# Making a table of angles by sine instead of by doubling, in a kernel that mixes an SSM and an MLP

## The chip, the cores and the metric

The kernel runs on one core of a Trainium2 chip. The metric is the device time of one execution in microseconds (us); the number for a kernel is the median of three such times. Before the change it was 549.61 us (549.30 to 549.72).

## The reference

Two branches read the same input x (2048 tokens of 1024 features, bf16) and are mixed by a gate per token. Cut to what matters:

```python
dt = exp(log_dt)
Lam_bar = exp(dt * Lam)                       # complex, one per channel, 1024 channels
B_bar = ((Lam_bar - 1) / Lam)[:, None] * Bmat
Bu = einsum("bld,pd->blp", x, B_bar)
for t in range(L):                            # 2048 steps
    h = Lam_bar * h + Bu[:, t]
a = 2 * einsum("blp,dp->bld", hs, Cmat).real + x * Dskip
b = gelu(layernorm(x) @ w1 + b1) @ w2 + b2
g = sigmoid((x * gate_w).sum(-1))
out = g * a + (1 - g) * b
```

## The kernel before, in words

The recurrence is split into size and angle. Lam_bar is R·exp(i·theta). In each stretch of T = 256 time steps the products Bu are turned by exp(-i·theta·t), so that a real scan with the factor R on VectorE (DVE, line 1471) is enough, and the result is turned back. For this a table of cos(theta·t) and sin(theta·t) is needed for t = 0 to 255 and 1024 channels: 128 partitions by 8 channels by 256 times, in f32 (region `E1`). From it the bf16 tables in `TABR` are written (lines 1056, 1058, 1071, 1073), which the DVE multiplications of the scan stage read (`ssm`, lines 1457 and 1460).

The table is made from theta in these steps. DVE brings dt·Im(Lam)/2pi into one turn (lines 966 to 969: `phi`, `ki`, `kf`, `ttr`), and a second copy that is a quarter turn ahead (lines 970 to 973), and clips both (975, 976). ScalarE (ACT) takes the sine of both (lines 977, 978). Then a recurrence of doublings on DVE: lines 996 to 998 give cos and sin of theta·2^k for k = 1 to 8 (three instructions each, 8 columns wide), and line 1024 doubles the table seven times (six instructions each, 8 to 512 columns wide), from column 128 upward, starting from a one and a zero that lines 1029 and 1031 set. ACT mirrors the upper half to the lower half (line 1047).

Matrix products run on TensorE (PE) in the groups of a Winograd-like scheme: a group has seven products `p1` to `p7` (lines 1090 and 1092), 4 matmuls of 512 columns each in the first stage. ACT copies PSUM banks out for it (`snap`, lines 1114 and 1115) and seeds a bank from another (line 1130); `p6` of a group waits for the seed, `p3` for the snap named s5. DVE writes other results out (line 1267) and makes sums and differences of operands in 16 bit (line 1180). The first group products read DVE's differences of x.

The order of the instructions on every engine is written by a planner in the kernel: it lists all steps with their dependencies, durations and priorities, simulates them, computes from the end backward when each step must start at the latest, subtracts a small random lead from that (`MIX` is the seed and the size of the lead), and orders each engine by it. Each engine then runs its list strictly in order, with semaphore waits. PE's list comes out in the order in which the code names the products.

Of the kernel before, what the change touches and what calls it, by code (L numbers as in the profile page):

```python
# [14 lines left out]
TWO_PI = 2.0 * math.pi  # L15
# [11 lines left out]
MIX = (12, 0.4)  # L27
# [19 lines left out]
def c_dve(N):  # L47
    return 0.09 + N / 960.0
# [547 lines left out]
def V(t, off, dims, npart=128):  # L596
    ps = 1
    for s in t.shape[1:]:
        ps *= s
    return bass.AP(t, off, [[ps, npart]] + [[a, b] for (a, b) in dims])  # L600


def build(nc, A_x, A_Lambda_re, A_Lambda_im, A_B_re, A_B_im, A_C_re, A_C_im, A_log_dt, A_Dskip,
# [25 lines left out]
    with es:  # L629
# [105 lines left out]
        for nm in ("DTC", "A", "TH", "R", "PHI", "KFX", "TTR", "T2", "KF2", "T3", "C1", "S1", "UR", "UI",  # L735
                   "Q", "Q2", "INV", "N1", "N2", "N3", "N4", "E20R", "E20I", "CC", "SS", "NMS"):
            alloc_cols(nm, PT)
        for k in range(1, LT + 1):
            alloc_cols("MC%d" % k, PT)
            alloc_cols("MS%d" % k, PT)  # L740
        col["MC0"] = col["C1"]
        col["MS0"] = col["S1"]
        b_cst["MC0"] = bc("C1")
        b_cst["MS0"] = bc("S1")
# [5 lines left out]
        def C(name, j=0, n=1):  # L750
            return V(CST, col[name] + j, [(1, n)])
# [201 lines left out]
        def dv(name, fn, reads, writes, dur=0.12, eng="dve", prio=(2.0, 0)):  # L953
            return g.add(eng, dur, prio, fn, reads=[bc(r) for r in reads], writes=[bc(w) for w in writes], name=name)
# [1043 lines left out]
```

## Time and profile before

| what | value |
|---|---|
| median of three runs | 549.61 us |
| the profiled execution, its own time | 549.65 us |
| span of its instructions | 547.8 us |
| PE busy | 541.2 us, 99% |
| DVE busy | 505.1 us, 92%, 870 instructions |
| ACT busy | 279.0 us, 51%, 466 instructions |
| POOL busy | 86.0 us, 16%, 146 instructions |
| granted TensorE clock | full in all 40 slices |

The span runs from the first to the last instruction of the program; 1.85 us of the time lie outside of it. Busy time is the union of an engine's instructions. PE's matmuls are pipelined, each is shown with 0.38 us although the next one starts 0.216 us later, and 47 of 2628 matmul records are missing, while all 2628 weight loads (PEld) are there. A weight load stands in the trace some 0.2 us ahead of its matmul, since it is fetched while the matmul before still runs.

### The profile page before, as it was taken

The numbers are of one execution on the slowest core, as the hardware profiler recorded it, in microseconds if no ns is written. First come the engines' busy times: TensorE is split into PE (matmuls) and PEld (weight loads), VectorE is DVE, ScalarE is ACT, GpSimd is POOL, SyncE is SP. The second block draws the span as 40 slices with busy tenths as digits, with TensorE's granted clock in tenths as the row PEclk, the third lists the DMA queues.
The fourth block names the chain that finished last, engine by engine and source line by source line (L and its number), as shares of the span: only waits on it lengthen the run. The fifth ranks groups of instructions, "written<-read, shape, count | busy, mean of one in ns | idle before, by whom it ended". The sixth has DMA issues, their size and how long they took to land.

```text
span 547.8 us, 7420 instructions
## 1 busy us (share of the span) xinstructions
PE 541.2 (99%) x2581; PEld 249.9 (46%) x2628; DVE 505.1 (92%) x870; ACT 279.0 (51%) x466; POOL 86.0 (16%) x146
## 2 busy tenths in 40 slices
PE   8999999999999999999999999999999999999998
PEld 6444444444444444444444444444444444444444
DVE  5997898999999999999999999999999999989884
ACT  3657988877764257763347762247663322111110
POOL 0134455610001110001210001120001100022000
PEclk9999999999999999999999999999999999999999
DMA  9999999959965155634778772977767997679621
GB/s 265 196 341 234 272 267 273 372 174 323 274 116 191 78 193 186 217 107 171 257 291 231 268 186 46 223 124 238 239 157 143 220 330 282 223 252 271 224 100 59
DMA packets 116448, 117.99 MB, mean 215 GB/s; under 512 B 72626, under 2 KB 94898, under 8 KB 115386
## 3 DMA queue, kind: packets, MB, share of 16 engines
q1 hardware_dynamic: 103792, 71.59, 46.7%
q0 software_dynamic: 12480, 45.90, 27.4%
q8 instruction: 21, 0.34, 0.3%
q14 instruction: 17, 0.14, 0.1%
q10 hardware_dynamic: 138, 0.02, 0.0%
HBM read 55.87 MB, written 45.37 MB: 185 GB/s over the span
## 4 chain that ended last, share of the span: by engine, by line
PE 98%; DMA 1%; issue 1%; SPq 0%; DVE 0%
PE ps L1092 72%; PE ps L1090 24%; DMA ar<-in_A_x_dram 1%; PE ps L935 0%; PE ps L1333 0%; PE ps L862 0%; PE ps L1161 0%; PE ps L838 0%; PE ps L912 0%; SPq L894 0%; SPq L808 0%; DVE ar L1783 0%; PE ps L947 0%
## 5 line engine op out<-in xcount | busy, mean ns | idle before, releaser
L1092 PE MATMUL ps<-ar 128*128 128x512 f16 (+1 forms) x1804 | 414.6, 379 | 2.2
L1092 PEld LDWEIGHTS ps<-ar 128*128 128x128 f16 (+1 forms) x1844 | 180.0, 98 | 218.5 <-ACT ar L1114 0.6
L1090 PE MATMUL ps<-ar 128*128 128x512 bf16 (+1 forms) x601 | 149.0, 379 | 0.3
L1180 DVE TENSOR_TENSOR ar<-ar 128x512 f16<-128x512 bf16 (+6 forms) x224 | 141.9, 663 | 0.8 <-ACT ar L870 0.3
L1090 PEld LDWEIGHTS ps<-ar 128*128 128x128 bf16 (+1 forms) x608 | 59.3, 98 | 71.1
L1471 DVE TENSOR_TENSOR_SCAN ar<-cst,init,ar 128x256 bf16<-128x256 f32 x128 | 88.6, 736 | 0.3
L1114 ACT ACTIVATE ar<-ps 128x512 f32<-128x512 f32 x102 | 60.4, 595 | 54.5 <-PE ps L1090 38.4
L1130 ACT ACTIVATE ps<-ps 128x512 f32<-128x512 f32 x67 | 38.9, 581 | 77.4 <-PE ps L1090 66.9
L1457 DVE TENSOR_TENSOR ar<-ar 128x2048 bf16<-128x2048 bf16 x64 | 77.1, 1218 | 0.0
L1115 ACT ACTIVATE ar<-ps,cst 128x512 f32<-128x512 f32 x32 | 22.0, 687 | 45.8 <-PE ps L1092 22.9
L1578 ACT ACTIVATE ar<-ps,cst 128x512 bf16<-128x512 f32 x56 | 38.4, 687 | 13.5 <-PE ps L1092 13.0
L1667 ACT ACTIVATE ar<-ps,cst 128x512 f32<-128x512 f32 x32 | 21.8, 687 | 45.0 <-PE ps L1092 45.0
L1582 DVE TENSOR_TENSOR ar<-ps,ar 128x512 f32<-128x512 f32 x56 | 38.1, 684 | 5.2 <-PE ps L1092 4.5
L1460 DVE TENSOR_TENSOR ar<-ar 128x1024 bf16<-128x1024 bf16 x64 | 42.3, 685 | 0.2
L1584 ACT ACTIVATE ar<-ar,cst 128x512 bf16<-128x512 f32 x56 | 39.7, 713 | 3.6 <-DVE ar L1582 3.6
L1198 POOL DMA_DIRECT2D scr_u<-ar x32 | 24.7, 774 | 56.2 <-ACT ar L1262 19.8
L1796 DVE SCALAR_TENSOR_TENSOR ar<-ps,cst,ar 128x512 bf16<-128x512 f32 x31 | 23.0, 747 | 8.8 <-PE ps L1092 8.7
L1489 POOL DMA_DIRECT2D scr_h<-ar x16 | 9.0, 563 | 125.4 <-DVE ar L1460 108.5
L1670 DVE SCALAR_TENSOR_TENSOR ar<-ps,cst,ar 128x512 f32<-128x512 f32 x32 | 23.7, 745 | 4.3 <-PE ps L1092 4.2
L1267 DVE TENSOR_TENSOR ar<-ps,ar 128x512 bf16<-128x512 f32 x30 | 20.5, 685 | 6.2 <-PE ps L1092 5.7
L1681 POOL DMA_DIRECT2D scr_ac<-ar x12 | 10.3, 888 | 78.6 <-DVE ar L1471 26.0
L1679 POOL DMA_DIRECT2D scr_ac<-ar x16 | 8.5, 532 | 79.6 <-DVE ar L1180 36.9
(121 smaller groups left out, 229.7 us busy)
## 6 DMA issues: line engine op xcount, KB each, us to landing
scr_ac<-ar POOLq DMA_DIRECT2D x28, 512.0 KB, 5.2
ar<-in_A_x_dram SPq DMA_DIRECT2D x32, 256.0 KB, 5.9
scr_u<-ar POOLq DMA_DIRECT2D x32, 256.0 KB, 5.1
ar<-scr_u SPq DMA_DIRECT2D x16, 512.0 KB, 4.7
scr_h<-ar POOLq DMA_DIRECT2D x16, 512.0 KB, 4.6
ar<-scr_h SPq DMA_DIRECT2D x8, 1024.0 KB, 6.6
ar<-in_B_w_dram SPq DMA_DIRECT2D x14, 512.0 KB, 4.7
ar<-in_B_w_dram SPq DMA_DIRECT2D x8, 896.0 KB, 7.6
```

Source lines behind the costliest of these rows:

```text
L1090: ins = e.matmul(V(PS[bk], 0, [(1, n)]), st[i].ap, mv[i].ap, start=(i == 0), stop=(i == K - 1))
L1092: ins = e.matmul(V(PS[bk], 0, [(1, n)]), st[i].ap, mv[i].ap, start=False, stop=(i == K - 1), skip_group_check=True)
L1114: return e.activation(o.ap, V(PS[bk], 0, [(1, 512)]), AF.Copy)
L1130: g.add("act", c_act(512), (pb[0], q - 2), lambda e: e.activation(V(PS[b], 0, [(1, 512)]), V(PS[a], 0, [(1, 512)]), AF.Copy), reads=[b_ps[ ...
L1180: g.add("dve", c_tt16(n), (pb[0], q), lambda e: e.tensor_tensor(o.ap, a.ap, b.ap, op), reads=[a, b], writes=[o], name=nm).slack = slack
L1198: g.dma((1.0, q), lambda e: e.dma_start(out=US[pt // 4, :, 4 * pr:4 * pr + 4, r0:r0 + T], in_=evv.ap), 2 * 128 * CH * 2, ssem("us", 2 * ks ...
L1457: g.add("dve", c_tt16(UE), pri(i), lambda e: e.tensor_tensor(o.ap, a.ap, tbl.ap, ALU.mult), reads=[a, tbl], writes=[o], name=nm + tag)
L1460: g.add("dve", c_tt16(UE // 2), pri(i), lambda e: e.tensor_tensor(o.ap, a.ap, b.ap, op), reads=[a, b], writes=[o], name=nm + tag)
L1471: lambda e, pt=pt, ri=ri, vin=vin, go=go: e.tensor_tensor_scan(go.ap, Cb("R", pt, T), vin.ap, V(INIT, pt * 2 + ri, [(1, 1)]), ALU.mult, AL ...
L1578: g.add("act", c_act(512, ap_operands=1), (10.0, q + 1), lambda e: e.activation(o.ap, V(PS[bk], 0, [(1, 512)]), AF.Gelu_apprx_tanh, bias=C ...
L1582: g.add("dve", c_dve(512), (10.0, q - 2), lambda e: e.tensor_tensor(sv.ap, V(PS[bk], 0, [(1, 512)]), sv.ap, ALU.add), reads=[b_ps[bk], sv] ...
L1584: g.add("act", c_act(512, psum=False, ap_operands=1), (10.0, q + 3), lambda e: e.activation(o.ap, sv.ap, AF.Gelu_apprx_tanh, bias=C("B1", ...
```

## The change

The sine and cosine are taken directly. One phase per channel (`TTR`, in turns) is multiplied on DVE by the column numbers 0 to 127, a row that GpSimd (POOL) writes by doubling into `ONESF`; it is brought into one turn by adding and subtracting 12582912, which rounds, and by one subtraction. ACT takes the sine of the whole upper half (1024 columns for each partition), and the cosine as 1 - 2·sin(half the angle)²: a sine, a square and a copy with scale and bias, all 1024 columns wide. The few columns that the other formulas need (theta, 128 theta and 256 theta) come from the same five steps on 24 columns. The 24 instructions of lines 996 to 998, the 42 of line 1024, the two memsets and the quarter-turn copy go. The planner's seed goes from 12 to 23.

```diff
-MIX = (12, 0.4)
+MIX = (23, 0.4)
...
-        dv("t2", ...0.25 added...)   dv ki2, kf2, t3, ttr_cl, t3_cl
-        dv("sin", lambda e: e.activation(C("S1", 0, n8), C("TTR", 0, n8), AF.Sin, scale=TWO_PI), ["TTR"], ["S1"], dur=0.3, eng="act", prio=P0).slack = 5.0
-        dv("cos", lambda e: e.activation(C("C1", 0, n8), C("T3", 0, n8), AF.Sin, scale=TWO_PI), ["T3"], ["C1"], dur=0.3, eng="act", prio=P0).slack = 5.0
+        PTURN = TWO_PI * (1.0 - 3e-7)
+        RND = 12582912.0
+        dv("x1", lambda e: e.tensor_copy(C("X1", 0, n8), C("TTR", 0, n8)), ["TTR"], ["X1"])
+        dv("x2", lambda e: e.tensor_scalar(C("X2", 0, n8), C("TTR", 0, n8), float(T // 2), None, ALU.mult), ["TTR"], ["X2"])
+        dv("x3", lambda e: e.tensor_scalar(C("X3", 0, n8), C("TTR", 0, n8), float(T), None, ALU.mult), ["TTR"], ["X3"])
+        dv("xk", lambda e: e.tensor_scalar(C("XK", 0, 3 * n8), C("X1", 0, 3 * n8), RND, RND, ALU.add, ALU.subtract), ["X1", "X2", "X3"], ["XK"])
+        dv("xr", lambda e: e.tensor_tensor(C("X1", 0, 3 * n8), C("X1", 0, 3 * n8), C("XK", 0, 3 * n8), ALU.subtract), ["X1", "X2", "X3", "XK"], ["X1"])
+        dv("sin", ...24 columns, AF.Sin...)  dv sinh, sinq (Square), cos (Copy)
...
-        for k in range(LT):
-            dv("cs%d" % k, ...)
-            dv("ms%d" % k, ...)
-            dv("mc%d" % k, ...)
...
-        g.add("dve", 0.12, PT1, lambda e, v=v: e.memset(v.ap, 1.0), writes=[v], name="e1r0")
-        g.add("dve", 0.12, PT1, lambda e, v=v: e.memset(v.ap, 0.0), writes=[v], name="e1i0")
+        g.add("pool", 0.2, P0, lambda e: e.memset(V(ONESF, 0, [(1, 1)]), 0.0), reads=[b_ident], writes=[b_ones], name="iota0")
         for k in range(LT - 1):
             n = 1 << k
-            tt("e1.%da" % k, ...)   and five more
+            g.add("pool", 0.3, P0, lambda e, n=n: e.tensor_scalar(V(ONESF, n, [(1, n)]), V(ONESF, 0, [(1, n)]), 1.0, float(n), ALU.mult, ALU.add), reads=[b_ones], writes=[b_ones], name="iota%d" % n)
+        ph = V(CST, col["TTR"], [(1, PT), (0, TH)])
+        g.add("dve", c_dve(PT * TH), PT1, lambda e: e.tensor_tensor(up0.ap, V(ONESF, 0, [(0, PT), (1, TH)]), ph, ALU.mult), ..., name="e1x")
+        g.add("dve", 0.75, PT1, lambda e: e.tensor_scalar(lo0.ap, up0.ap, RND, RND, ALU.add, ALU.subtract), ..., name="e1k")
+        g.add("dve", c_dve(PT * TH), PT1, lambda e: e.tensor_tensor(up0.ap, up0.ap, lo0.ap, ALU.subtract), ..., name="e1r")
+        g.add("act", ca, PT1, lambda e: e.activation(up1.ap, up0.ap, AF.Sin, scale=PTURN), ..., name="e1s")
+        g.add("act", ca, PT1, lambda e: e.activation(lo1.ap, up0.ap, AF.Sin, scale=PTURN / 2), ..., name="e1h")
+        g.add("act", ca, PT1, lambda e: e.activation(lo1.ap, lo1.ap, AF.Square, scale=math.sqrt(2.0)), ..., name="e1q")
+        g.add("act", ca, PT1, lambda e: e.activation(up0.ap, lo1.ap, AF.Copy, scale=-1.0, bias=1.0), ..., name="e1c")
```

The change takes lines out, so a line behind it has a smaller number now: 1114, 1130, 1180, 1262 and 1267 of before are 1106, 1122, 1172, 1254 and 1259.

DVE, where the phases are ready (from `ttr`, line 969 before and 964 now, to the first operand sums). Before:

```order
L969 TENSOR_TENSOR cst<-cst 128x8
L970 TENSOR_SCALAR cst<-cst 128x8
L975 TENSOR_SCALAR cst<-cst 128x8
L971 CAST ki<-cst 128x8
L972 CAST cst<-ki 128x8
L973 TENSOR_TENSOR cst<-cst 128x8
L976 TENSOR_SCALAR cst<-cst 128x8
L1180 TENSOR_TENSOR ar<-ar 128x512 x2
L1180 TENSOR_TENSOR ar<-ar 128x2048
```

Now:

```order
L964 TENSOR_TENSOR cst<-cst 128x8
L967 COPY cst<-cst 128x8
L968 TENSOR_SCALAR cst<-cst 128x8
L969 TENSOR_SCALAR cst<-cst 128x8
L1027 TENSOR_TENSOR ar<-onesf,cst 128x8x128
L1172 TENSOR_TENSOR ar<-ar 128x512
L1172 TENSOR_TENSOR ar<-ar 128x2048
```

The six small steps of the quarter turn have become three (`x1` to `x3`), and `e1x` (L1027), 1024 columns wide, stands ahead of the operand sums.

DVE, behind those sums, with the first results of group u1.0 written out (L1267, now L1259). Before:

```order
L1267 TENSOR_TENSOR ar<-ps,ar 128x512
L997 SCALAR_TENSOR_TENSOR cst<-cst 128x8
L996 TENSOR_TENSOR cst<-cst 128x16
L1267 TENSOR_TENSOR ar<-ps,ar 128x512
L998 TENSOR_TENSOR cst<-cst 128x8
L1024 TENSOR_TENSOR ar<-ar,cst 128x8
```

Now:

```order
L970 TENSOR_SCALAR cst<-cst 128x24
L1259 TENSOR_TENSOR ar<-ps,ar 128x512
L971 TENSOR_TENSOR cst<-cst 128x24
L1028 TENSOR_SCALAR ar<-ar 128x8x128
L1259 TENSOR_TENSOR ar<-ps,ar 128x512
L1029 TENSOR_TENSOR ar<-ar 128x8x128
L1172 TENSOR_TENSOR ar<-ar 128x512
L1259 TENSOR_TENSOR ar<-ps,ar 128x512
L1172 TENSOR_TENSOR ar<-ar 128x512 x4
L1259 TENSOR_TENSOR ar<-ps,ar 128x512
```

The doublings no longer stand between the results; `xk`, `xr` (L970, L971) and the wide `e1k`, `e1r` (L1028, L1029) do.

ACT, from the snaps of groups u1.0 and u2.0 (L1114, now L1106) to the seed of group u0.1 (L1130, now L1122). Before:

```order
L1114 ACTIVATE ar<-ps 128x512 x2
L977 ACT_TABLE_LOAD
L977 ACTIVATE cst<-cst 128x8
L978 ACTIVATE cst<-cst 128x8
L1114 ACTIVATE ar<-ps 128x512 x2
L1130 ACTIVATE ps<-ps 128x512
L1262 ACTIVATE ar<-ps 128x512
L1114 ACTIVATE ar<-ps 128x512 x2
L1262 ACTIVATE ar<-ps 128x512 x2
L1130 ACTIVATE ps<-ps 128x512
```

Now, without the last two rows of that stretch, which are `e1c` (L1034) and the seed:

```order
L1106 ACTIVATE ar<-ps 128x512 x4
L1031 ACT_TABLE_LOAD
L1031 ACTIVATE ar<-ar 128x8x128
L1122 ACTIVATE ps<-ps 128x512
L1032 ACTIVATE ar<-ar 128x8x128
L973 ACTIVATE cst<-cst 128x24
L1254 ACTIVATE ar<-ps 128x512
L974 ACTIVATE cst<-cst 128x24
L1106 ACTIVATE ar<-ps 128x512 x2
L975 ACTIVATE cst<-cst 128x24
L1033 ACTIVATE ar<-ar 128x8x128
L1254 ACTIVATE ar<-ps 128x512 x2
```

The load of the sine's table stands two snaps later, and the wide `e1s` (L1031) now stands ahead of the seed of group u3.0, `e1h` (L1032) and two small ones ahead of its snaps, `e1q` (L1033) and `e1c` ahead of the seed of u0.1. PE's own list is the same in both kernels.

## Rows read from the trace of the kernel before

**Rows 1.** Chain that ended last, by engine, and PE's own waits (total, times, longest).
```profile
PE 98%; DMA 1%; issue 1%; SPq 0%; DVE 0%
...
PE ps L882 <- DVE ar L1031: 1.2, 1, 1.2
PE ps L838 <- DMA ar<-in_A_x_dram: 0.2, 1, 0.2
```

**Rows 2.** Timeline of the first and last microseconds: start, us, engine, line, what.
```profile
0.91 0.27 DVE L885 MEMSET ar<- 128x256 uint32 x1 [0.91 <-PEq L1983]
...
543.34 1.93 PE L1161 MATMUL ps<-ar 128*128 128x256 bf16 x24
```

**Rows 3.** Timeline from 104.5 us.
```profile
104.53 0.53 PEld L1092 LDWEIGHTS ps<-ar 128*128 128x128 f16 x3
...
104.81 1.28 DVE L1267 TENSOR_TENSOR ar<-ps,ar 128x512 bf16<-128x512 f32 x2
...
105.60 0.99 PEld L1092 LDWEIGHTS ps<-ar 128*128 128x128 bf16 x6 [0.55 <-issue]
```

**Rows 4.** Groups of lines on DVE that go: count, busy us, mean ns.
```profile
L1024 DVE TENSOR_TENSOR ar<-ar,cst 128x8 f32<-128x8 f32 (+6 forms) x28 | 7.2, 304 | 0.0
L1024 DVE TENSOR_TENSOR ar<-ar 128x8 f32<-128x8 f32 (+6 forms) x14 | 4.0, 304 | 0.0
```

**Rows 5.** DVE groups of one shape each, near to what is added.
```profile
L1180 DVE TENSOR_TENSOR ar<-ar 128x4096 f16<-128x4096 bf16 x4 | 9.1, 2284 | 0.0
L1307 DVE TENSOR_SCALAR ar<-ar,cst 128x1024 bf16<-128x1024 bf16 x16 | 8.6, 581 | 1.9 <-POOL cst L1302 1.8
...
L1024 DVE TENSOR_TENSOR ar<-ar,cst 128x512 f32<-128x512 f32 x4 | 2.6, 684 | 0.0
L1024 DVE TENSOR_TENSOR ar<-ar,cst 128x256 f32<-128x256 f32 x4 | 1.4, 419 | 0.0
```

**Rows 6.** Timeline of DVE, 15 to 30 us.
```profile
15.71 0.17 DVE L970 TENSOR_SCALAR cst<-cst 128x8 f32<-128x8 f32 x1
...
17.07 6.31 DVE L1180 TENSOR_TENSOR ar<-ar 128x512 f16<-128x512 bf16 x9 [0.30 <-ACT ar L870]
23.29 0.69 DVE L1267 TENSOR_TENSOR ar<-ps,ar 128x512 bf16<-128x512 f32 x1
...
29.94 0.68 DVE L1267 TENSOR_TENSOR ar<-ps,ar 128x512 bf16<-128x512 f32 x1
```

**Rows 7.** Timeline of PE, 20.5 to 39 us.
```profile
21.36 1.46 PE L1092 MATMUL ps<-ar 128*128 128x512 f16 x6
...
30.07 3.62 PE L1092 MATMUL ps<-ar 128*128 128x512 f16 x15
...
38.04 1.25 PE L1092 MATMUL ps<-ar 128*128 128x512 f16 x5
```

**Rows 8.** ACT groups of one shape: wide copies, and the sine of 8 columns.
```profile
L1056 ACT ACTIVATE ar<-ar 128x1024 bf16<-128x1024 f32 x2 | 2.1, 1048 | 0.0
...
L977 ACT ACTIVATE cst<-cst 128x8 f32<-128x8 f32 x1 | 0.2, 208 | 0.0
```

**Rows 9.** Timeline of ACT, 22 to 27 us.
```profile
22.43 0.60 ACT L1114 ACTIVATE ar<-ps 128x512 f32<-128x512 f32 x1 [0.27 <-PE ps L1092]
23.04 1.28 ACT L977 ACT_TABLE_LOAD   x1
24.34 0.21 ACT L977 ACTIVATE cst<-cst 128x8 f32<-128x8 f32 x1
...
25.95 0.60 ACT L1114 ACTIVATE ar<-ps 128x512 f32<-128x512 f32 x1 [0.27 <-PE ps L1092]
```

**Rows 10.** Timeline and groups of POOL: last memset, first DMA, dearest small operation.
```profile
1.32 0.10 POOL L1003 MEMSET init<- 128x16 f32 x1
20.73 1.72 POOL L1198 DMA_DIRECT2D scr_u<-ar  x2 [19.30 <-DMA ar<-in_A_x_dram]
...
L1301 POOL TENSOR_TENSOR cst<-cst 128x4 f32<-128x4 f32 x4 | 5.1, 1268 | 0.2
```

More of the change, by code (lines that the diff above doesn't have):

```diff
@@ L734, in build @@
         assert ncol[0] == NROW
-        for nm in ("DTC", "A", "TH", "R", "PHI", "KFX", "TTR", "T2", "KF2", "T3", "C1", "S1", "UR", "UI",
+        for nm in ("DTC", "A", "TH", "R", "PHI", "KFX", "TTR", "T2", "KF2", "T3", "UR", "UI",
                    "Q", "Q2", "INV", "N1", "N2", "N3", "N4", "E20R", "E20I", "CC", "SS", "NMS"):
             alloc_cols(nm, PT)
[L738 to L744, printed above, removed]
+        for nm in ("C1", "MC%d" % (LT - 1), "MC%d" % LT, "S1", "MS%d" % (LT - 1), "MS%d" % LT, "X1", "X2", "X3", "XK", "XK2", "XK3", "XH", "XH2", "XH3"):
+            alloc_cols(nm, PT)
         alloc_cols("MHALF", TT)
@@ new lines, in build @@
+        dv("xk", lambda e: e.tensor_scalar(C("XK", 0, 3 * n8), C("X1", 0, 3 * n8), RND, RND, ALU.add, ALU.subtract), ["X1", "X2", "X3"], ["XK"])
+        dv("xr", lambda e: e.tensor_tensor(C("X1", 0, 3 * n8), C("X1", 0, 3 * n8), C("XK", 0, 3 * n8), ALU.subtract), ["X1", "X2", "X3", "XK"], ["X1"])
+        trig_s, trig_c = ["S1", "MS%d" % (LT - 1), "MS%d" % LT], ["C1", "MC%d" % (LT - 1), "MC%d" % LT]
+        dv("sin", lambda e: e.activation(C("S1", 0, 3 * n8), C("X1", 0, 3 * n8), AF.Sin, scale=PTURN), ["X1"], trig_s, dur=0.3, eng="act").slack = 5.0
@@ L979, in build @@
+        dv("sinh", lambda e: e.activation(C("XH", 0, 3 * n8), C("X1", 0, 3 * n8), AF.Sin, scale=PTURN / 2), ["X1"], ["XH"], dur=0.3, eng="act").slack = 5.0
+        dv("sinq", lambda e: e.activation(C("XH", 0, 3 * n8), C("XH", 0, 3 * n8), AF.Square, scale=math.sqrt(2.0)), ["XH"], ["XH"], dur=0.3, eng="act")
+        dv("cos", lambda e: e.activation(C("C1", 0, 3 * n8), C("XH", 0, 3 * n8), AF.Copy, scale=-1.0, bias=1.0), ["XH"], trig_c, dur=0.3, eng="act")
         dv("ur0", lambda e: e.tensor_tensor(C("UR", 0, n8), C("R", 0, n8), C("C1", 0, n8), ALU.mult), ["R", "C1"], ["UR"])
@@ L1027, in build @@
         TH = T // 2
-        v = w1(0, TH, 1)
-        g.add("dve", 0.12, PT1, lambda e, v=v: e.memset(v.ap, 1.0), writes=[v], name="e1r0")
-        v = w1(1, TH, 1)
-        g.add("dve", 0.12, PT1, lambda e, v=v: e.memset(v.ap, 0.0), writes=[v], name="e1i0")
+        up0, up1, lo0, lo1 = w1(0, TH, TH), w1(1, TH, TH), w1(0, 0, TH), w1(1, 0, TH)
+        g.add("pool", 0.2, P0, lambda e: e.memset(V(ONESF, 0, [(1, 1)]), 0.0), reads=[b_ident], writes=[b_ones], name="iota0")
         for k in range(LT - 1):
@@ L1041, in build @@
-            tt("e1.%de" % k, PT1, o0, o0.ap, t0.ap, ALU.add, [o0, t0], dc)
-            tt("e1.%df" % k, PT1, o1, o1.ap, t1.ap, ALU.subtract, [o1, t1], dc)
+            g.add("pool", 0.3, P0, lambda e, n=n: e.tensor_scalar(V(ONESF, n, [(1, n)]), V(ONESF, 0, [(1, n)]), 1.0, float(n), ALU.mult, ALU.add), reads=[b_ones], writes=[b_ones], name="iota%d" % n)
+        ph = V(CST, col["TTR"], [(1, PT), (0, TH)])
+        g.add("dve", c_dve(PT * TH), PT1, lambda e: e.tensor_tensor(up0.ap, V(ONESF, 0, [(0, PT), (1, TH)]), ph, ALU.mult), reads=[b_ones, bc("TTR")], writes=[up0], name="e1x")
@@ new lines, in build @@
+        g.add("dve", 0.75, PT1, lambda e: e.tensor_scalar(lo0.ap, up0.ap, RND, RND, ALU.add, ALU.subtract), reads=[up0], writes=[lo0], name="e1k")
+        g.add("dve", c_dve(PT * TH), PT1, lambda e: e.tensor_tensor(up0.ap, up0.ap, lo0.ap, ALU.subtract), reads=[up0, lo0], writes=[up0], name="e1r")
+        ca = c_act(PT * TH, psum=False)
+        g.add("act", ca, PT1, lambda e: e.activation(up1.ap, up0.ap, AF.Sin, scale=PTURN), reads=[up0], writes=[up1], name="e1s")
+        g.add("act", ca, PT1, lambda e: e.activation(lo1.ap, up0.ap, AF.Sin, scale=PTURN / 2), reads=[up0], writes=[lo1], name="e1h")
@@ L1043, in build @@
+        g.add("act", ca, PT1, lambda e: e.activation(lo1.ap, lo1.ap, AF.Square, scale=math.sqrt(2.0)), reads=[lo1], writes=[lo1], name="e1q")
+        g.add("act", ca, PT1, lambda e: e.activation(up0.ap, lo1.ap, AF.Copy, scale=-1.0, bias=1.0), reads=[lo1], writes=[up0], name="e1c")
         NTAB = PT * T
```

18 lines of the change are left out of this document (removed).

## The prediction

> **What bounds the kernel now.** I read the chain that ended last first, since it names the engine whose work adds up to the time: 98% of it is PE [rows 1]. Next come PE's own waits. There are two in the whole execution, 1.2 us at the start and 0.2 us for a DMA in the opening [rows 1]. The last matmuls stand at 543.34 us and run 1.93 us, so PE ends at 545.27, and 2.57 us of output DMA follow to the end of the span [rows 2]. From the second of them on to 545.3 us PE has work in hand nearly all the time; its list is the same in both kernels. The time can fall only by the few tenths that PE does lose, and rise only where a result from another engine reaches PE later than the matmul in front of it ends.
>
> DVE is 92% busy, which invites the reading that work taken from DVE is time won. The chain says otherwise: DVE has 0% of it [rows 1]. A busy engine that always delivers before PE asks costs nothing.
>
> The third reading is of the weight loads, which show small delays that the waits leave out. At 104.53 us three loads follow each other at 0.216 us, the third thus at 104.96, and the next was due at 105.17 but stands at 105.60 [rows 3]. It is 0.43 us late, of which some 0.2 us are covered by the lead of a load over its matmul, so PE lost about 0.23 us. What it waited for is the first of the two DVE results from 104.81 us on [rows 3].
>
> **The change, part by part.**
>
> What goes from DVE: the 42 instructions of the doublings, 7.2 + 4.0 = 11.2 us [rows 4], and 32 small ones (24 for the multiples of theta, six for the quarter turn and two memsets), at the 0.17 us of such an instruction [rows 6] some 5.4 us. Together 16.6 us. What comes: five small ones, 0.85 us, and three wide ones. Line 1024 took 684 ns for 512 columns and 419 for 256 in f32 [rows 5], 1.035 ns a column, so `e1x` and `e1r` with 1024 columns take 684 + 512 x 1.035 = 1214 ns each. For `e1k`, one f32 input and two constants, the nearest row is the tensor-scalar of 1024 columns in bf16, 581 ns [rows 5]; I take 0.65 us. Added: 0.85 + 2.43 + 0.65 = 3.9 us, net -12.7 us of DVE time. On PE's path that is zero, except at 105 us. There DVE hands over late; its work for the scan can begin earlier now, and the 0.23 us should go. This is the only gain that I count. Its bounds are 0 (the new order may be as tight there) and 0.23; I take 0.23, since the removed work is many times that.
>
> `e1x` stands ahead of the operand sums that PE waits for. Before, the first replaced step started at 15.71 us and the sums at 17.07, after 0.30 us of waiting for ACT [rows 6]. Now three small independent steps take 15.71 to about 15.95 (such instructions follow each other at 0.08 us when they don't depend), `e1x` runs to 15.95 + 1.21 = 17.16, and the next may enter 0.08 us before that end. So the sums start at about 17.1, where ACT lets them start anyway. The second difference of x is needed at 21.36 [rows 7]. In the new order it is the fourth of the sums. The nine sums, four of 2048 columns and five of 512, took 6.31 us [rows 6], about 1.13 and 0.34 us each, so it ends at 17.1 + 2 x 0.34 + 2 x 1.13 + 0.1 = 20.1. That is 1.2 us early: zero. Behind the sums DVE now has `xk`, `xr`, `e1k`, `e1r`, three results of groups u1.0 and u2.0 and five more sums before the second result of u2.0. From 23.29 us [rows 6]: 0.6 + 0.1 + 0.6 + 0.6 + 1.13 + 0.34 + 0.6 + 4 x 0.34 = 5.3 us, so it starts at 28.6 to 29.2; before, it started at 29.94 [rows 6]. PE needs it for the second group of four in the stretch from 30.07, at 30.93 [rows 7]. So DVE is ahead: zero again. The durations have a lower bound of 0 and an upper one in the widest DVE instruction that the trace has, 2.28 us [rows 5]. With 2.28 us for `e1x` and `e1r`, and 1.21 for `e1k`, the second result of u2.0 comes 1.07 + 1.07 + 0.56 = 2.7 us later than worked out, ends at 31.9 to 32.6 instead of 30.9, and PE loses 1.0 to 1.7 us. Between these ends the nearest row is f32 of 512 columns, and I keep 1.21.
>
> On ACT four wide instructions come. The copy of 1024 f32 columns took 1048 ns [rows 8]; a sine of 8 columns took 208 ns [rows 8], about what any instruction of that width takes, so a wide sine at the price of a wide copy is the nearest reading, 1.05 us, bounded below by 0.2 and above, far away, by the 2.28 us of DVE's widest. The table load is still one, 1.28 us, only later. The snap at 25.95 ends at 26.55 [rows 9]; the load runs to 27.85, `e1s` to 28.9, and the seed of u3.0 (0.58 us, overlapping its forerunner by 0.1) ends at 29.4. PE needs it at 30.07 [rows 7]: 0.6 us to spare. Then `e1h`, two small ones and one copy put the snap s5 of u3.0 at 30.95 to 31.55; PE needs it for the fourth group of that stretch, at 30.07 + 3 x 0.865 = 32.66, with 1.1 us to spare. Then come `e1q`, two copies, `e1c` and the seed of u0.1, which ends at 35.65; PE needs it at 38.04 [rows 7], 2.4 us to spare. All three are hidden by the matmuls of the groups in front. What is queued behind the wide ones are just these seeds and snaps. Sum: zero.
>
> The Trainium skill's page "ScalarE: Activation LUTs", section "What ACT_TABLE_LOAD costs", speaks against this place: a switch of tables costs a drain of about 1380 ns beside the load of 1283. In the trace the load starts at 23.04, when the snap of 22.43 has just ended, and the sine runs at 24.34 [rows 9], so the load shows and no drain does. By the page's figure as an estimate the seed of u3.0 would be 1.38 - 0.6 = 0.8 us late and the time 550.2; by the row it is on time, and I go by the row. The same page, in its step-by-step part, says that all functions run at one element per cycle; no run here shows it for a wide sine, and by it the sum stays as it is.
>
> On POOL eight small operations write the column numbers. POOL's last memset starts at 1.32 us and its first DMA waits until 20.73 [rows 10]. Even at the dearest small operation, 1.27 us [rows 10], eight end at 1.42 + 8 x 1.27 = 11.6, before `e1x` at 15.95; the lower bound is 0 and changes nothing.
>
> The two memsets at the start look like a gain, because PE's first wait is put down to the second of them (L1031) [rows 1]. But PE's first product needs the memset of line 885, which ends at 0.91 + 0.27 = 1.18 us [rows 2], and PE starts 0.06 us later. Should it start earlier, the DMA wait that follows takes it back. Zero.
>
> Sum: 549.65 - 0.23 = 549.4 us against the profiled execution's own time, which lies 0.04 us above the median of the runs, so 549.4 stands for both.
>
> **The rivals.**
>
> Slower, by ACT: the wide instructions on ACT cost twice the copy, 2.1 us each. For it: no row shows a wide sine or square in f32, and ACT is full from 26 to 38 us in the new order. Against: the narrow sine's duration. The first takes 1.05 - 0.6 = 0.45 us from PE; with the second, s5 is 2.1 - 0.45 - 1.1 = 0.55 late; with the other two the seed of u0.1 is 4.2 - 1.0 - 2.4 = 0.8 late. Total 1.8 us, 551.2 us. It decides the sign from about 1.9 us each, where the same steps give 0.25 + 0.35 + 0.5 = 1.1 us.
>
> Slower, by DVE: the wide f32 instructions at their upper bound, 549.4 + 1.0 to 1.7, 550.4 to 551.1 us. For it: `e1x` reads a row repeated by channel and a phase repeated by column, which no row has both of. Against: line 1024 reads one operand repeated too, at 684 ns.
>
> Faster, since DVE is the bound: 549.65 - 12.7 = 536.9 us. For it the 92%; against it the 0% of the chain.
>
> New order elsewhere: the new seed draws DVE's, ACT's and the queues' orders anew over the whole kernel. One late result can cost a few tenths, as at 105 us; two or three such, 0.6 us, give 550.0 us.
>
> **How the numbers follow.** A measurement of this kernel can tell about 0.2%, 1.1 us, from no change. Chances: the forecast 0.72, new order elsewhere 0.13, slower by ACT 0.07, slower by DVE 0.06, DVE as the bound 0.02. Faster by over 0.2% is the last alone, with a bit for unforeseen gains in the opening: 0.03. Slower is ACT's rival, half of DVE's, 0.03, and 0.01 of the reordering: 0.11. The rest, 0.86, is no change. The range goes from 548.9, what is left if PE loses nothing after the opening, to 550.6, which takes in the reordering, the drain and the nearer end of the DVE bound.
>
> **What would show it.** Right: PE still at 98% or more of the chain, wide sines near 1.05 us, `e1x` ending near 17.2 us with the sums following at once, seeds at 29.4 and 35.7 us with no idle PE at 30.1, 32.7 and 38.0, one load of the sine's table without a pause behind it, DVE's busy time down by 12 us, no late load at 105 us. Wrong: PE waiting for ACT between 30 and 38 us, for DVE between 20 and 33 us, or a last matmul that moves by over 1 us.

## The result and the profile after

The changed kernel takes 551.15 us, the median of 22 executions; the kernel before took 549.61 us in 22 executions beside it (549.21 to 550.20). The ratio is 1.0051, with a 95% interval from 1.0031 to 1.0070. Ratios, here and below, are of mean times and leave out executions over 1.5% above the fastest of the same kernel (three of the 22 here); the ratio of the two medians is 1.0028. The forecast was 549.4 us with a range that ended at 550.6, so the kernel came out slower, and above the range.

The median hides that there are two groups: 14 executions lie between 550.42 and 551.44 us, the other 8 between 554.05 and 561.93. The kernel before never went above 550.75 in any of its runs for this study. So two things have to be found: about one microsecond that every execution loses, and some 3 to 11 more that some lose.

The profile shows an execution of the first group, 550.72 us with a span of 548.5. The busy time by engine and the chain that ended last, which answer to [rows 1]:

```profile
PE 542.9 (99%) x2628; PEld 249.2 (45%) x2628; DVE 496.3 (90%) x804; ACT 281.3 (51%) x472; POOL 89.7 (16%) x154
...
PE 97%; POOL 1%; DMA 1%; issue 1%; ACT 0%; DVE 0%; SPq 0%; DVEq 0%; ACTq 0%
```

PE still carries the chain, but POOL, which had no share of it, now has 1%. PE's waits (total, times, longest) have a new member, the middle line:

```profile
PE ps L877 <- DVE gwc L1308: 1.2, 1, 1.2
PE ps L1084 <- DVE ar L1259: 1.1, 1, 1.1
PE ps L833 <- DMA ar<-in_A_x_dram: 0.7, 1, 0.7
```

It stands where I had counted a gain. The weight loads around 105 us, which answer to [rows 3], and the last matmuls, which answer to [rows 2]:

```profile
104.02 0.74 PEld L1084 LDWEIGHTS ps<-ar 128*128 128x128 f16 x4
106.28 1.21 PEld L1084 LDWEIGHTS ps<-ar 128*128 128x128 bf16 x7 [1.52 <-issue]
...
544.02 1.93 PE L1153 MATMUL ps<-ar 128*128 128x256 bf16 x24
```

Four loads from 104.02 at 0.216 us make the fifth due at 104.88; it stands at 106.28, 1.40 us late, where it was 0.43 late before. So PE loses 0.97 us more here. Up to 30 us it is 0.29 us ahead (the stretch of 30.07 in [rows 7] starts at 29.78), and the last matmuls move by the difference, from 543.34 to 544.02. That is 0.68 us of the 1.07 between the two profiled executions (549.65 and 550.72 us). The rest lies outside of the span, 2.2 us here and 1.85 before, and no run shows why.

Why the DVE result (L1259) is late is read from DVE and POOL at that time. DVE first, then POOL:

```profile
98.43 1.22 DVE L1449 TENSOR_TENSOR ar<-ar 128x2048 bf16<-128x2048 bf16 x1
...
102.31 0.43 DVE L1172 TENSOR_TENSOR ar<-ar 128x512 f16<-128x512 bf16 x1
104.48 1.09 DVE L1299 TENSOR_SCALAR ar<-ar,cst 128x1024 bf16<-128x1024 bf16 x2 [1.75 <-POOL cst L1294]
105.49 0.67 DVE L1259 TENSOR_TENSOR ar<-ps,ar 128x512 bf16<-128x512 f32 x1
```

```profile
99.63 3.15 POOL L1290 TENSOR_SCALAR cst<-cst 128x4 f32<-128x4 f32 x1 [0.65 <-ACT ar L1279]
102.87 0.20 POOL L1292 TENSOR_TENSOR cst<-cst 128x4 f32<-128x4 f32 x1
103.14 1.03 POOL L1293 TENSOR_TENSOR cst<-cst 128x4 f32<-128x4 f32 x1
104.25 0.20 POOL L1294 TENSOR_TENSOR cst<-cst 128x4 f32<-128x4 f32 x1
```

POOL's operation on line 1290, four columns wide, takes 3.15 us and ends at 102.78, 0.04 us after DVE's unbroken series of operations with two operands in SBUF (98.43 to 102.74). Three more small ones follow. DVE's next instruction in its order, the layer norm of line 1299, waits 1.75 us for the last of them, and the result that PE wants stands behind the layer norm. In the old order a layer norm (L1307, at 102.07 us) stood ahead of that result too, but POOL's operations for it had ended at 102.03 us, so it did not wait.

What I priced in the opening came out as forecast. ACT and DVE there answer to [rows 8, 9] and [rows 6]:

```profile
26.28 1.28 ACT L1031 ACT_TABLE_LOAD   x1
27.57 1.06 ACT L1031 ACTIVATE ar<-ar 128x1024 f32<-128x1024 f32 x1
28.54 0.58 ACT L1122 ACTIVATE ps<-ps 128x512 f32<-128x512 f32 x1
...
34.73 0.62 ACT L1122 ACTIVATE ps<-ps 128x512 f32<-128x512 f32 x1
```

```profile
15.80 1.22 DVE L1027 TENSOR_TENSOR ar<-onesf,cst 128x1024 f32<-128x1024 f32 x1
16.93 5.97 DVE L1172 TENSOR_TENSOR ar<-ar 128x512 f16<-128x512 bf16 x8
...
29.12 0.69 DVE L1259 TENSOR_TENSOR ar<-ps,ar 128x512 bf16<-128x512 f32 x1 [0.43 <-PE ps L1084]
```

The wide sine takes 1.06 us, the seeds end at 29.12 and 35.35 us, and PE waits for none of it.

### The profile page after: what moved, and what is told of

It is laid out like the page before. It is cut to its first block, busy times and chain, and to the rows that moved or that the text cites. A ratio compares the mean times of both kernels' runs of the same rounds, so it can differ in the third digit from the quotient of the medians.

```text
span 548.5 us, 7417 instructions
## 1 busy us (share of the span) xinstructions
PE 542.9 (99%) x2628; PEld 249.2 (45%) x2628; DVE 496.3 (90%) x804; ACT 281.3 (51%) x472; POOL 89.7 (16%) x154
## 4 chain that ended last, share of the span: by engine, by line
PE 97%; POOL 1%; DMA 1%; issue 1%; ACT 0%; DVE 0%; SPq 0%; DVEq 0%; ACTq 0%
PE ps L1084 72%; PE ps L1082 23%; DMA ar<-in_A_x_dram 1%; POOL cst L1290 1%; PE ps L930 0%; PE ps L1325 0%; PE ps L857 0%; PE ps L1153 0%; PE ps L833 0%; ACT ar L1279 0%; POOL cst L1293 0%; DVE ar L1259 0%; PE ps L907 0%; SPq L889 0%; SPq L803 0%
## 5 line engine op out<-in xcount | busy, mean ns | idle before, releaser
L1172 DVE TENSOR_TENSOR ar<-ar 128x512 f16<-128x512 bf16 (+7 forms) x224 | 141.8, 667 | 1.1 <-DMA ar<-in_A_x_dram 0.8
L1106 ACT ACTIVATE ar<-ps 128x512 f32<-128x512 f32 x102 | 60.2, 595 | 60.1 <-PE ps L1082 42.8
L1122 ACT ACTIVATE ps<-ps 128x512 f32<-128x512 f32 x67 | 39.0, 582 | 78.1 <-PE ps L1082 73.1
L1570 ACT ACTIVATE ar<-ps,cst 128x512 bf16<-128x512 f32 x56 | 38.4, 687 | 10.6 <-PE ps L1084 10.1
L1259 DVE TENSOR_TENSOR ar<-ps,ar 128x512 bf16<-128x512 f32 x30 | 20.6, 688 | 15.3 <-PE ps L1084 15.0
L1662 DVE SCALAR_TENSOR_TENSOR ar<-ps,cst,ar 128x512 f32<-128x512 f32 x32 | 23.9, 749 | 3.1 <-PE ps L1084 1.3
L1673 POOL DMA_DIRECT2D scr_ac<-ar x12 | 10.3, 861 | 78.7 <-ACT ar L1659 40.1
```

The source lines that it names most:

```text
L1106: return e.activation(o.ap, V(PS[bk], 0, [(1, 512)]), AF.Copy)
L1122: g.add("act", c_act(512), (pb[0], q - 2), lambda e: e.activation(V(PS[b], 0, [(1, 512)]), V(PS[a], 0, [(1, 512)]), AF.Copy), reads=[b_ps[ ...
L1172: g.add("dve", c_tt16(n), (pb[0], q), lambda e: e.tensor_tensor(o.ap, a.ap, b.ap, op), reads=[a, b], writes=[o], name=nm).slack = slack
L1570: g.add("act", c_act(512, ap_operands=1), (10.0, q + 1), lambda e: e.activation(o.ap, V(PS[bk], 0, [(1, 512)]), AF.Gelu_apprx_tanh, bias=C ...
```

## The experiments

The planner's lists can be edited after it has made them, and the waits follow from the lists. Most edits below are such moves, a few lines behind `g.schedule(passes=3)`. `u7.1.1` is the DVE result that PE waited for, `ln_norm12` the layer norm in front of it, `ln_ex23` the POOL operation of line 1290. `xns0` to `xns15` are POOL's stores of the layer norm's rows (`scr_xn`), those named `us` its stores of other results (`scr_u`), and `xnT0.0.0` to `xnT0.1.1` the four loads that bring the rows back transposed.

**e1: the changed kernel again.** No edit.

> The changed kernel once more, to see whether the long executions recur and, if the profiled one is among them, where they lose their time. Theory A (one place): an execution is longer by what PE idles at 105 to 107 us, where a small GpSimd operation (line 1290) waits for VectorE's stream to end; the shortest executions stand near 550.4 us, and in a long one the idle stretch of PE is several us and the granted clock falls behind it. Theory B (spread): the long ones lose time in many places, or at the clock alone, with PE idle for no more than 1.2 us at 106 us. Expected by both: a median of 550.5 to 552 us; by A a profile whose surplus over the span of before, 547.8 us, stands in one stretch.

Measured: 566.82, 556.87, 550.74 and 551.03 us, ratio 1.0057 [1.0006, 1.0108]. The profile fell on the execution of 566.82, and shows what the second group loses. My expectation of a single place fell. The stall at 106 us is there as before, but two more waits come behind it:

```profile
PE ps L1082 <- DVE ar L1172: 7.3, 1, 7.3
...
PE ps L1084 <- DVE ar L1172: 4.8, 1, 4.8
```

These DVE sums wait for the transposed loads of the layer norm's rows (`scr_xn`, issued by SyncE with DMA_TRANSPOSE). The DMAs of 60 to 125 us, with the median time from issue to landing in us, first of this execution, then of the one of 550.72:

```profile
scr_xn<-ar POOLq DMA_DIRECT2D x16, 256.0 KB, 6.7
...
ar<-scr_xn SPq DMA_TRANSPOSE x4, 17.0
```

```profile
scr_xn<-ar POOLq DMA_DIRECT2D x16, 256.0 KB, 5.4
...
ar<-scr_xn SPq DMA_TRANSPOSE x4, 6.6
```

One by one, the four loads take 8.2, 15.1, 18.8 and 20.6 us, in the execution of 550.72 they take 7.1, 10.7, 5.7 and 6.1. While the second is under way here (82.7 to 97.8 us), the trace has nothing but POOL's stores beside it, and the four stores issued just behind it take 13.5 us each.

And PE's clock falls behind the wait. In the windows, the first two numbers behind the stretch are its length and PE's busy time, the last three the granted clock, the DMA share and GB/s:

```profile
110.00:120.00 10.00, 2.70 (x11) 0.91 (x9) 2.29 (x3) 2.08 (x3) 0.45 (x1) 0.82 1.22 153
120.00:130.00 10.00, 4.97 (x12) 1.64 (x12) 5.84 (x7) 1.99 (x4) 3.63 (x6) 0.50 1.05 351
130.00:140.00 10.00, 10.00 (x47) 4.51 (x46) 9.49 (x18) 6.08 (x11) 0.94 (x2) 1.00 0.65 213
```

After 7.3 us without work PE runs at half clock (0.50, the level of 1.2 GHz) until about 130 us. The two waits are 12.1 us of the 16.1 by which this execution is longer than the one of 550.74; about 4 are left for the matmuls at half clock.

**e2: u7.1.0 and u7.1.1 ahead of the layer norm.** It tells whether the POOL operation costs the first microsecond.

```python
dq = g.order["dve"]; at = {t.name: t for t in dq}
for nm in ("u7.1.0", "u7.1.1"):
    dq.remove(at[nm]); dq.insert(dq.index(at["ln_norm12"]), at[nm])
```

> The changed kernel, with two entries of VectorE's list moved: the two results of group u7.0 (u7.1.0 and u7.1.1, line 1259) stand ahead of the normalisation of row 12 (line 1299) that waits for GpSimd, all else word for word. Theory A: PE no longer stands behind that wait, its late load at 106 us goes, the time falls to 549.4 us plus what lies newly outside of the span, 549.4 to 549.9 us, and no execution is longer than 550.5. Theory B (the sine's own instructions, or the new order as a whole): the median stays at 550.5 to 551.5 us with long ones among them.

Measured: 549.85, 549.69, 549.94 and 568.04 us; the ratio is 1.0001 [0.9985, 1.0017]. The late load is gone, and with it the microsecond; the long executions are not, where I had expected none above 550.5. They have another cause.

**e3 and e4: sine and seed apart.** e3 is the changed kernel with `MIX = (12, 0.4)`, e4 the kernel before with `MIX = (23, 0.4)`.

> The sine with the old seed, 12, of the planner's draw. If the time is lost by the place that the new draw gave to the waiting normalisation (theory A), another draw with the same sine loses something else: here the normalisation of row 12 stands after three sums and not behind a scan multiplication, so no loss at 106 us is expected, 549.3 to 549.9 us. If the sine's instructions cost the time wherever they stand (theory B), it is 550.5 us or more here too.

> The kernel before, doublings and all, with the new seed, 23. Theory A: the loss belongs to an order, not to the sine; this order differs again (the table's bf16 rows stand between the normalisations), and the time is 549.3 to 550.0 us, or longer by what a GpSimd wait costs at some other place. Theory B: 549.6 us, as before.

Measured: e3 549.96 us (549.66 to 550.47), ratio 1.0005 [0.9990, 1.0019]; e4 560.39 us (559.03 to 565.01), ratio 1.0208 [1.0168, 1.0248]. With the sine and the old order nothing is lost in these four executions; the new order alone costs 10 us without the sine, though at a place that the changed kernel doesn't have. PE's waits in e4 and the DMA behind them, `ctB22`, one transposed load of C, at 405 to 460 us:

```profile
PE ps L1092 <- DVE ar L1670: 5.0, 1, 5.0
PE ps L1092 <- DVE ar L1180: 2.0, 1, 2.0
```

```profile
ar<-in_A_C_im_dram SPq DMA_TRANSPOSE x1, 23.9
```

In the drawn order `ctB22` stands behind `hg0`, a load that waits until 430 us, and so runs beside POOL's stores `acs1.1` to `acs1.3`. Again a transposed load beside POOL's stores: the theory for the second group (A) is that the two slow each other.

**e5: DVE waits for the POOL operation.** It tells whether POOL is shut out by DVE's series or slow by itself.

```python
at = {t.name: t for t in g.tasks}
at["nb0.0"].deps.add(at["ln_ex23"])
```

> The changed kernel; the first of DVE's multiplications in the stream at 98.4 us (nb0.0, line 1449) is made to wait for GpSimd's small operation on line 1290, which took 3.15 us beside that stream. Theory A, DVE's operations with two operands in SBUF shut GpSimd out until a gap comes: line 1290 takes 0.2 to 0.6 us, since DVE stands idle beside it, and it is one of the three small ones after it (lines 1292 to 1294) that now takes 2 us or more and ends within 0.2 us of the end of DVE's stream. Rival B, the operation on line 1290 is slow by itself, for instance because it follows five DMA issues: it takes about 3 us again while DVE is idle, and the other three take 0.2, 1.0 and 0.2 us as before. The time under A is about 552 (DVE's idle 1.5 us come on top of the 1.2 at 106 us).

Measured: 549.62 us in one execution, beside 549.52 for the kernel before. POOL:

```profile
99.79 0.47 POOL L1290 TENSOR_SCALAR cst<-cst 128x4 f32<-128x4 f32 x1 [0.58 <-ACT ar L1279]
100.35 1.23 POOL L1292 TENSOR_TENSOR cst<-cst 128x4 f32<-128x4 f32 x1
101.66 1.09 POOL L1293 TENSOR_TENSOR cst<-cst 128x4 f32<-128x4 f32 x1
102.83 0.36 POOL L1294 TENSOR_TENSOR cst<-cst 128x4 f32<-128x4 f32 x1
```

Rival B fell: the same operation takes 0.47 us. Theory A is half right. Line 1292 now takes 1.23 us instead of 0.20 and ends 0.06 us after a DVE operation (100.30 to 101.52), as the theory has it, but none takes 2 us: POOL came in between two DVE operations, while in the changed kernel it had missed every such change. The four end 1.26 us earlier, and instead of the loss of 1.5 us that I expected, DVE's pause of 0.09 us (100.21 to 100.30) repaid the whole microsecond, as far as one execution can tell. What decides whether POOL gets in at such a change stays open.

**e6 and e7: one place in SyncE's list.** In e4's kernel `ctB22` is put ahead of `hg0`; in the kernel before, with its own seed, behind it.

```python
sq = g.order["sp"]; at = {t.name: t for t in sq}
sq.remove(at["ctB22"]); sq.insert(sq.index(at["hg0"]), at["ctB22"])      # e6
sq.remove(at["ctB22"]); sq.insert(sq.index(at["hg0"]) + 1, at["ctB22"])  # e7
```

> The doubling kernel with seed 23, which took 560.4 us; on SyncE's queue the transposed load ctB22 (from C, 128 partitions) is put ahead of the load hg0, so that it no longer stands behind hg0's wait and is issued at about 412 us instead of 430. Theory A, a transposed load and GpSimd's stores that run at the same time slow each other down by a factor of two to four: ctB22 lands in 6 to 7 us instead of 23.9, the stores acs1.1 to acs1.3 in 3 to 6 instead of 8 to 18.5, PE's idle stretch at 450 to 460 us goes and the time is 549.5 to 551. Rival B, the loss comes from another place of the drawn order (hg0 or the stores are late by themselves): the time stays near 560. Rival C, half of it goes: 554 to 556.

> The kernel before, with its own seed, and only ctB22 put one place later on SyncE's queue, behind hg0. Theory A (transposed load and GpSimd's stores slow each other): ctB22 is issued at about 424 to 430 us, takes over 15 us, the stores beside it over 8, PE idles for some microseconds at 450 to 460, and the time is 556 to 561. Rival B (the place does no harm by itself): ctB22 lands in 6 to 7 us and the time stays within 549.3 to 550.3.

Measured: e6 550.93 us (550.61 to 551.67), ratio 1.0025 [1.0016, 1.0034]; e7 564.78 us (561.10 to 570.43), ratio 1.025 [1.0221, 1.0279]. The load and the stores `scr_ac` beside it, landing time, first of e6, then of the kernel before, then of e7; with e6 and e7 stands a window:

```profile
scr_ac<-ar POOLq DMA_DIRECT2D x4, 512.0 KB, 7.8
...
ar<-in_A_C_im_dram SPq DMA_TRANSPOSE x1, 6.8
...
445.00:455.00 10.00, 8.42 (x39) 3.64 (x39) 10.00 (x12) 3.29 (x6) 0.00 (x0) 1.00 1.00 380
```

```profile
scr_ac<-ar POOLq DMA_DIRECT2D x4, 512.0 KB, 6.7
...
ar<-in_A_C_im_dram SPq DMA_TRANSPOSE x1, 6.7
```

```profile
scr_ac<-ar POOLq DMA_DIRECT2D x4, 512.0 KB, 16.3
...
ar<-in_A_C_im_dram SPq DMA_TRANSPOSE x1, 33.9
...
445.00:455.00 10.00, 0.80 (x4) 0.18 (x2) 0.36 (x1) 0.00 (x0) 0.00 (x0) 0.79 1.18 64
```

A is right in both directions: the load goes from 23.9 us in e4 to 6.8 in e6, and from 6.7 in the kernel before to 33.9 in e7, and the time follows. While load and stores run together in e7 the DMA engines are shown as busy (1.18) and move 64 GB/s. The load `hg0` is not what slows `ctB22`: it landed at 436.4 us, and from then to 456.5 only `ctB22` and stores were under way. Some numbers were off. I expected `acs1.1` to `acs1.3` at 3 to 6 us without the transposed load beside them, and in e6 they took 7.7 to 10.1. e7 lost more than the 556 to 561 us that I expected. And e6 keeps 1.4 us over the kernel before; its trace has a PE wait of 1.5 us for a DVE sum (L1180), which no run follows up.

**e8 and e9: stores kept away from the transposed loads in the changed kernel.** Both with e2's edit. e8 holds POOL's stores until the second of the four loads has landed, e9 holds them for each pair and moves POOL's small operations ahead.

```python
pq.remove(ap["ln_nmr1"]); pq.insert(pq.index(ap["us5.0.0"]), ap["ln_nmr1"])
ap["us5.0.0"].deps.add(next(t for t in g.order["sp"] if t.name == "xnT0.0.1"))  # e8
...
ap["xns4"].deps.add(sp["xnT0.0.1"]); ap["xns8"].deps.add(sp["xnT0.1.1"])          # e9
```

> The changed kernel with the two DVE operations u7.1.0 and u7.1.1 ahead of the layer norm (as in the run that brought 549.9), and GpSimd's stores from us5.0.0 on (at 79.9 us) made to wait until the second transposed load xnT0.0.1 has landed, so that transposes and stores no longer run at the same time at 80 to 90 us. Theory A (their overlap sets off the long executions): xnT0.0.0 and xnT0.0.1 land in 5 to 8 us, and all executions lie within 549.3 to 550.6; with 14 of 22 executions of the changed kernel in the short group, six short ones in a row would come by chance in 7 of 100 cases. Rival B (long executions have another cause): one or more of six lie above 553. Rival C: holding the stores costs by itself, over 0.5 us in every execution.

> The changed kernel with u7.1.0 and u7.1.1 ahead of the layer norm as in e2; besides, GpSimd's stores xns4 to xns7 wait until xnT0.0.1 has landed, and the stores from xns8 on until xnT0.1.1 has landed (the layer norm's small operations are moved ahead of them), so that neither pair of transposed loads runs beside stores; in e8 the second pair still did, and its loads took 9.8 and 10.3 us. Theory A (that overlap sets off the long executions): all four loads land in 5 to 7.5 us and all executions lie within 549.3 to 550.8. Rival B (they have another cause): some lie above 553. Rival C: the stores that are held make DVE or PE wait in every execution, a steady loss of 0.5 us or more without long ones.

Measured: e8 557.6 us (550.78 to 564.88, four of six above 553), ratio 1.0113 [1.0071, 1.0156]. B seemed to win, but e8 had moved the meeting: in its profile the first pair landed in 6.2 and 6.1 us, the second, now late, ran beside stores and took 9.8 and 10.3. That profile is of the execution of 551.75 us; where the long ones of e8 lose their time is not shown. e9: 564.61 to 565.35 in five executions, ratio 1.0281 [1.0268, 1.0294]. The loads, and PE's largest wait:

```profile
ar<-scr_xn SPq DMA_TRANSPOSE x4, 5.2
```

```profile
PE ps L1082 <- DMA ar<-in_B_w_dram: 12.4, 1, 12.4
```

Kept apart, the loads take 5.2 us in the median, and the spread shrinks to 0.7 us. The price is rival C, far above what I thought: the held stores go out in one bunch, and a load of weights that stands on SyncE's queue behind a load which waits for them comes 12.4 us late, every time.

**e10 and e11: control, and the meeting brought about in the kernel before.** e10 is e2's kernel again. e11 is the kernel before with one wait:

```python
first = lambda e, nm: next(t for t in g.order[e] if t.name == nm)
first("sp", "xnT0.0.0").deps.add(first("pool", "xns4"))
```

> The kernel of e2 once more, beside e9 on the same chip, as its control. Theory A: some of about six executions lie above 553 (one of four did before, and 14 of 36 of the changed kernel and its copies); the rest at 549.7 to 550.0. If none does, e9 tells little.

> The kernel before, doubling and seed 12 as they were; only the first transposed load of the layer norm's rows (xnT0.0.0, issued at 64.8 us) is made to wait for the store xns4, so that it and xnT0.0.1 run at 81 to 90 us beside the stores xns5 to xns7, us5.0.0 and us5.0.1, as in the changed kernel. Theory A: xnT0.0.1 takes 9 to 12 us, and some of about six executions lie above 553, as none of 46 of the kernel before does; the others stay at 549.3 to 550.3. Rival B (the long executions belong to the sine): all stay at 549.3 to 550.5.

Measured: e10 549.82 us, eight of twelve executions from 548.71 to 550.24 and four from 555.17 to 575.53, ratio 1.0010 [0.9991, 1.0029]. e11 565.71 us (561.95 to 571.22), ratio 1.0282 [1.0240, 1.0324]: all six executions long, where I had expected some. But the pair of loads that is hit is not the one that I named. The first pair, which the edit moved beside the stores, lands in 8.4 and 6.0 us (8.5 and 7.7 in the kernel before), not in 9 to 12. The second, issued at 90.7 and 98.4 us instead of 86.3 and 88.4, lands in 15.1 and 20.2 instead of 5.2 and 6.7; SyncE needs 22.19 us only to issue it, 5.07 in the kernel before. First e11, then before:

```profile
80.72 8.74 SPq L1513 DMA_TRANSPOSE ar<-scr_xn  x2
90.68 22.19 SPq L1513 DMA_TRANSPOSE ar<-scr_xn  x2
```

```profile
64.75 8.05 SPq L1513 DMA_TRANSPOSE ar<-scr_xn  x2
86.34 5.07 SPq L1513 DMA_TRANSPOSE ar<-scr_xn  x2
```

So the long executions don't belong to the sine as such: one wait brings them about without it. Nor is it enough that a load runs beside stores. In the kernel before, POOL issues five stores from 89.6 to 92.6 us, beside the second pair, and that pair lands on time. What differs when a meeting slows both is not shown.

What moves the loads in the changed kernel is read from ACT. The first of its four sums of squares for the layer norm (L1287 before, L1279 after), and the copy of the finished table to bf16 (L1056, L1048), before and then after:

```profile
38.65 1.05 ACT L1287 ACTIVATE ar<-ar 128x1024 bf16<-128x1024 bf16 x1
...
59.46 1.05 ACT L1056 ACTIVATE ar<-ar 128x1024 bf16<-128x1024 f32 x1
```

```profile
37.59 1.08 ACT L1048 ACTIVATE ar<-ar 128x1024 bf16<-128x1024 f32 x1
57.84 1.05 ACT L1279 ACTIVATE ar<-ar 128x1024 bf16<-128x1024 bf16 x1
```

With the sine the table is ready 22 us earlier; its followers take ACT's free time from 35 to 58 us, and the layer norm comes 19 us later. With it its first rows are stored 15 us later, from 72 us, and the first pair of transposed loads is issued at 79.8 us instead of 64.8, beside six stores that POOL issues from 79.9 to 84.4; the second pair follows at 91.9 instead of 86.3. e3, with the old seed, has its sums from 57.54 us too, so this is the sine's doing and not the seed's. Its loads stand at the same place and land in 8.2 to 12.3 us, yet none of its four executions was long. At the changed kernel's rate (10 long ones in 26) that comes by chance in (16/26)^4 = 14% of cases, so e3 leaves open whether the old seed is free of them.

**e12: the layer norm early again.** e2's kernel, with ACT's sums back at 40 to 53 us and the followers of the table behind them. `put` moves entries of an engine's list behind or ahead of a named one.

```python
for anchor, names in (("ze", "ln_sq0"), ("su_u1.1", "ln_sq1"), ..., ("seed_u2.1", "ln_sq2"), ..., ("su_u2.1", "ln_sq3"), ...):
    put("act", anchor, names, 1)
...
put("pool", "us2.1.0", "xns0 xns1 xns2 xns3", 1)
...
put("sp", "w1_0", "xnT0.0.0 xnT0.0.1", 1)
```

> The changed kernel with u7.1.0 and u7.1.1 ahead of the layer norm as in e2, and the first layer norm chunk put back to where the kernel before has it: ScalarE's four sums of squares (ln_sq0 to ln_sq3, 58 to 69 us in the changed kernel, since ScalarE is filled with the wide sines and the tables after them up to 58 us) at 40 to 53 us, the steps e2t0, e2t1, e2r and ne2i of the second table that stood there later, ma0.0 later, the rows' stores xns0 to xns3 at 57 to 60 us and the loads xnT0.0.0 and xnT0.0.1 at 64 to 74 us, away from the stores xns4 to xns7. Theory A (the late layer norm brought transposed loads and stores together, and that makes the long executions): no execution above 551, and the others within 549.2 to 550.5. Rival B (another cause): one or more of about six above 553, as 4 of 12 in e10. Rival C: the moved steps make PE wait at 42 to 66 us, a steady loss of 0.5 us or more.

Measured: 549.58 us, eleven executions from 549.21 to 550.21, none long; ratio 1.0003 [0.9994, 1.0012]. With five long ones among the sixteen of e2 and e10, eleven short ones in a row would come by chance in (11/16)^11 = 1.6% of cases. The first pair of loads is back at 65 us. First the changed kernel, whose two pairs (79.8 and 91.9 us) the view shows as one row, since SyncE issues nothing between them, then e12:

```profile
79.78 17.29 SPq L1505 DMA_TRANSPOSE ar<-scr_xn  x4
```

```profile
65.21 8.39 SPq L1505 DMA_TRANSPOSE ar<-scr_xn  x2
88.29 6.48 SPq L1505 DMA_TRANSPOSE ar<-scr_xn  x2
```

A stands as far as the place goes: with the layer norm late the long executions come, with it early they don't. e12 moves many steps besides, and also has stores beside its loads (four near the first pair), so it does not show which of them matter. Of the versions with the sine that ran more than once it is the fastest, and it equals the kernel before.

## Why the prediction was wrong

- **What bounds the kernel.** Right in the main: PE has 97% of the chain, where 98 or more was asked for, and 8.8 us less of DVE time brought nothing.
- **DVE's net time, -12.7 us.** Mis-sized, measured -8.8. I added up parts, while busy time is a union, in which small instructions lie over each other and their neighbours. What went was put at 16.6 us; it adds up to 17.9, but only 11.7 us of the union were its alone. What came was put at 3.9 us; it adds up to 4.0 and fills 3.1 of the union. PE does not feel either.
- **The opening on DVE, ACT and POOL: zero.** Right in each step: `e1x` 1.22 us, the sums from 16.93, the second result of u2.0 at 29.12, the wide sine 1.06, the seeds at 29.12 and 35.35, no pause at the table load (the sine begins 0.01 us behind it). The Trainium skill's page "ScalarE: Activation LUTs", section "What ACT_TABLE_LOAD costs", has a drain of about 1380 ns beside the load; it does not show here either.
- **The gain of 0.23 us at 105 us, "Its bounds are 0 ... and 0.23".** Failed. The bounds looked only at how much work goes ahead of the late result, and not at what stands in front of it in the new order: a layer norm that waits for POOL. I read [rows 10] for POOL's dearest small operation, 1.27 us, and [rows 5] show 1.8 us of DVE waiting for POOL (L1307 on L1302), but I did not ask what stood behind that wait. Measured: 0.97 us lost at that place (e2 gives it back in three of four executions, e5 in its one).
- **"What is queued behind the wide ones are just these seeds and snaps. Sum: zero."** Failed, and it cost most in the executions that it hit. It holds up to 38 us. Behind them stood the table's followers and behind these the layer norm, 19 us later; this moved transposed loads into a burst of stores, and in 10 of 26 executions they slowed each other (8 of the 22 here, 3 to 11 us). One moved wait makes long executions without the sine (e11), and an early layer norm takes them away with it (e12). I had shown that PE does not wait for a moved step, but not followed the step to the DMAs that it releases.
- **The rival "new order elsewhere", 0.6 us at 0.13.** It is the kind of thing that came true, mis-sized by far: I took a late result for a few tenths of a microsecond, and one place in a DMA queue is worth 9 to 15 (e4 against e6, e7 against the kernel before). The seed alone was not the cause, though: the late layer norm comes with the sine (e3).
- **The rivals by ACT's and DVE's wide instructions.** Fell, as the rows on the opening show.

## What to carry to other kernels

When a step moves, follow it to the transfers that it releases and ask what else the DMA engines do then; this kernel, bound by one engine, lost most by late loads, not by slower instructions. An operation that becomes early is not free either, since its followers can take the place of others on the same engine. And where the executions fall into two groups, take a profile of each before looking for a cause: here there were two.

## What the runs showed of the hardware

A DMA transpose issued by SyncE and stores issued by GpSimd can slow each other severely: one load took 6.7 us without them (the kernel before) and 33.9 beside stores of 512 KB (e7), and the median of the four stores `scr_ac` in that stretch went from 6.7 to 16.3, while the engines were shown as busy (1.18) and moved 64 GB/s. They need not: in the kernel before two such loads beside five stores took 5.2 and 6.7 us. The Trainium skill's page "DMA: Bandwidth & Descriptors", section "Rules for kernel authors", says that a transpose next to ordinary DMAs needs nothing. That row is about data that two transposes corrupt; for the time, these runs show that it can need care. Why the same list collapses in 10 of 26 executions of the changed kernel and not in the others stays open.

A GpSimd operation of four columns took 3.15 us beside DVE operations with two SBUF operands, and ended 0.04 us after them. The Trainium skill's page "SBUF — State Buffer", section "SBUF: two separate sides", has it so: a GpSimd operation that reads SBUF and a DVE operation with two SBUF inputs take a shared port pair as an exclusive lock, the first for its whole instruction, and the other blocks. The trace agrees, and adds that the loser can miss several changes of instruction in a row: POOL's operation started at 99.63 us and got in at none of DVE's changes from 99.90 to 102.31.

PE's granted clock stayed at 1.00 behind a wait of 1.1 us (the changed kernel, 550.72 us), and was found at 0.50 behind the one of 7.3 us in e1.
